# Seven block products for eight in the last FFN, and GpSimd sums for the first batch's inverse step

## The chip, the cores and the metric

One core of a Trainium2 chip runs the whole kernel. The metric is the time of one execution on the device, in microseconds (us), as a median of several executions. A profile shows one execution; its span is some 2 us shorter than the time reported for that same execution (2409.3 for 2411.47 us before), and executions of one kernel differ by a few us.

## The reference, cut to what matters

```python
# x, v: (4, 12544, 128); D = 128, d_ff = 768
h_filt = (np.maximum(pos_emb @ w1, 0.0) @ w2) * window[:, None]
y = irfft(rfft(x * v, 2 * S, axis=1) * rfft(h_filt, 2 * S, axis=0))[:, :S]   # long convolution
x = (x * y).reshape(B * S, D)                                               # 50176 tokens
h = np.maximum(np.maximum(x @ moe_w1, x @ moe_w2), x @ moe_w3)
return h @ moe_w_out
```

Everything is float32. The convolution of one batch is a chain of matrix products with constant tables; the FFN of one batch runs beside the convolution of the next. Only the FFN of the fourth batch runs alone.

## The kernel before

A batch's FFN has 32 tiles of 4 x 98 = 392 tokens. `t_last` makes the last inverse step of the convolution for a tile and multiplies by x; `up` makes one of six blocks of 128 hidden values; `down` multiplies it by w_out and adds up. The first of the three weight matrices is folded out: max(a, b, c) is written as a plus a maximum with differences, so `lin` carries the linear part and two up-products remain.

```python
def halves_mm(out, lhsT, rhs, start, stop):          # a product as two half-array products
    for h in range(2):
        nc.tensor.matmul(out[64 * h:64 * h + 64], lhsT[:, 64 * h:64 * h + 64], rhs, ...)

def t_last(i):                                       # i = (batch, tile)
    ...
    if i[0] == 0:                                    # batch 0: two 98-column products, accumulated
        for s in range(4):
            for c in range(2):
                halves_mm(y[:, s, :], zt[:, c, s * D:(s + 1) * D], f4[:, c, :], s == 0 and c == 0, c == 1)
    else:                                            # later: zt holds sums and differences of pairs of k1
        for s in range(4):
            for a in range(2):
                halves_mm(y[:, s, a * h:a * h + h], zt[:, a, s * D:(s + 1) * D], f4p[:, a, :], ...)
    ... # g = y * xT on VectorE

def up(i, f):
    halves_mm(pa[:, 0:N], w_sb[1][:, f * P:(f + 1) * P], rhs, True, True)
    nc.scalar.activation(h[:], pa[:, 0:N], Relu)
    halves_mm(pb[:, 0:N], w_sb[2][:, f * P:(f + 1) * P], rhs, True, True)
    nc.vector.tensor_tensor(out=h[:], in0=h[:], in1=pb[:, 0:N], op=ALU.max)
    return h

def down(i, f, h):
    if f == 0:
        halves_mm(pos_[i][:, 0:N], lin[:], gs[i], True, False)
    halves_mm(pos_[i][:, 0:N], wo_sb[:, f, :], h[:], False, f == NF - 1)
    ... # after the sixth: copy by ScalarE, DMA to outT from ScalarE's queue

for n, (b, i) in enumerate(tiles):                   # all 128 tiles
    for f in range(NF):
        ... # loads for tile n + 2
        h = up((b, i), f)
        if late is not None:
            down(*late)
        late = ((b, i), f, h)
        if f == 3 and n + 1 < len(tiles):
            t_last(tiles[n + 1])
        run(beside.pop(s, ()))                       # steps of the next batch's convolution
```

## Time and profile before

| | |
|---|---|
| time, median of 4 | 2414.89 us (2413.1 to 2417.17) |
| profiled span | 2409.3 us |
| TensorE busy | 99% |
| GpSimd busy, whole span / last batch's FFN | 13% / 0% |
| last inverse step of a tile, batch 0 / later | 1.36 / 0.92 us |
| period of a tile in the last batch | 13.44 us |

The prediction below shows the lines that carry this. A line of the chain of waits is "start, length, what"; a line of the table by stage is a stretch, its length, busy time of PE, PEld, DVE, ACT and POOL with instruction counts, the granted TensorE clock, DMA share and GB/s.

### The profile page before, as it was taken

Reading aid. Unit: us, or ns where it says so; the run is one execution under the profiler, and the core shown is the slowest. Engines: PE = TensorE matmul, PEld = TensorE weight load, DVE = VectorE, ACT = ScalarE, POOL = GpSimd, SP = SyncE. Lnnn points to the kernel's source line nnn. Section 1 sums busy time; section 2 is a strip of 40 time slices with the busy share of each in tenths; the row PEclk is TensorE's granted clock in tenths of the full one; section 3 lists DMA queues with packets and bytes.
Section 4 is the critical chain, followed back from the end, with each engine's and each line's share of the span. In section 5 each row is a group of like instructions: output and inputs, shape, how many; then the busy total and the mean of one; then the engine's idle time right before and its main releaser. Section 6 shows DMA issues by size and latency. Waiting matters only on the chain.

```text
span 2409.3 us, 63290 instructions
## 1 busy us (share of the span) xinstructions
PE 2393.4 (99%) x26089; PEld 1463.2 (61%) x26089; DVE 1286.4 (53%) x2719; ACT 1026.7 (43%) x1981; POOL 314.2 (13%) x349
## 2 busy tenths in 40 slices
PE   9999999999999999999999999999999999999999
PEld 8988866655555556666656546666665654444444
DVE  5588834466666645446666644446666642222222
ACT  2688834444444434444444424444444432222222
POOL 2022211011111101101111111101111100000000
PEclk9999999999999999999999999999999999999999
DMA  7778879767767659967777859968777742222221
GB/s 171 179 240 266 278 167 179 162 190 196 214 194 211 175 125 187 182 174 207 219 207 215 219 124 182 189 162 213 214 215 209 215 113 61 55 62 53 64 53 36
DMA packets 544553, 408.21 MB, mean 169 GB/s; under 512 B 390244, under 2 KB 436381, under 8 KB 544265
## 3 DMA queue, kind: packets, MB, share of 16 engines
q1 hardware_dynamic: 421760, 315.25, 53.8%
q10 hardware_dynamic: 117129, 74.31, 10.7%
q0 software_dynamic: 5376, 14.62, 2.1%
q8 instruction: 205, 3.36, 0.6%
q14 instruction: 83, 0.68, 0.1%
HBM read 295.76 MB, written 84.67 MB: 158 GB/s over the span
## 4 chain that ended last, share of the span: by engine, by line
PE 97%; DMA 1%; ACT 1%; DVE 0%; issue 0%; SPq 0%; ACTq 0%; POOL 0%; DVEq 0%
PE ops L132 24%; PE pb L132 21%; PE pa L132 21%; PE ps L132 13%; PE ps L141 7%; PE yps L132 5%; PE sps L688 3%; PE pm L303 1%; PE gps L674 1%; PE pst L341 1%; PE pw L132 1%; DMA hd<-ht 1%; ACT ht L693 0%; DMA xT<-in_x_dram 0%; DVE xt L424 0%
## 5 line engine op out<-in xcount | busy, mean ns | idle before, releaser
L548 DVE TENSOR_TENSOR hid<-hid,pb 128x392 f32<-128x392 f32 x768 | 431.8, 562 | 789.4 <-PE pb L132 510.2
L545 ACT ACTIVATE hid<-pa 128x392 f32<-128x392 f32 x768 | 381.9, 498 | 799.3 <-PE pa L132 630.1
L132 PE MATMUL pa<-gt,w_sb 128*64 128x392 f32 x3072 | 640.7, 493 | 1.1 <-DVE gt L533 1.1
L132 PE MATMUL pb<-gt,w_sb 128*64 128x392 f32 x3072 | 639.6, 492 | 1.4 <-ACT hid L545 1.2
L132 PE MATMUL ops<-hid,wo_sb 128*64 128x392 f32 x3072 | 639.5, 492 | 0.1
L132 PEld LDWEIGHTS pb<-gt,w_sb 128*64 128x64 f32 x3072 | 225.8, 137 | 283.0 <-issue 257.1
L132 PEld LDWEIGHTS ops<-hid,wo_sb 128*64 128x64 f32 x3072 | 227.1, 137 | 278.9 <-issue 228.8
L424 POOL TENSOR_TENSOR xt<-xt,xs 128x512 f32<-128x512 f32 x135 | 172.5, 1278 | 969.6 <-DVE xs L423 778.7
L132 PEld LDWEIGHTS pa<-gt,w_sb 128*64 128x64 f32 x3072 | 201.8, 137 | 111.3 <-issue 67.4
L141 PEld LDWEIGHTS ps<-f,uT 98*64 98x64 f32 x4096 | 178.0, 137 | 47.4 <-issue 44.7
L132 PEld LDWEIGHTS ps<-ab,wt 128*64 128x64 f32 x2880 | 168.4, 137 | 52.4 <-issue 26.8
L132 PE MATMUL ps<-ab,wt 128*64 128x128 f32 x2880 | 190.9, 274 | 1.8 <-DVE ab L431 1.7
L132 PEld LDWEIGHTS ps<-spec,wt 128*64 128x64 f32 x2880 | 168.0, 137 | 37.8 <-issue 34.2
L132 PE MATMUL ps<-spec,wt 128*64 128x128 f32 x2880 | 189.5, 273 | 1.4 <-issue 1.4
L141 PE MATMUL ps<-f,uT 98*64 98x90 f32 x4096 | 188.0, 241 | 0.0
L449 DVE TENSOR_TENSOR zs<-ps,z 128x256 f32<-128x256 f32 x270 | 102.0, 419 | 96.6 <-ACT z L447 94.3
L413 ACT ACTIVATE xs<-xt 64x512 f32<-64x512 f32 x180 | 113.1, 628 | 71.1 <-DVE xt L158 58.9
L431 DVE TENSOR_TENSOR ab<-xt 128x256 f32<-128x256 f32 x360 | 136.0, 419 | 1.6
L419 DVE TENSOR_TENSOR xt<-xt,ht 128x512 f32<-128x512 f32 x180 | 124.2, 690 | 15.6 <-ACT ht L693 15.2
L356 POOL COPY planes<-ut 128x784 uint16<-128x784 uint16 x90 | 76.2, 847 | 426.5 <-DVE ut L336 301.1
L145 ACT COPY spec<-ps 128x360 f32<-128x360 f32 (+1 forms) x132 | 71.8, 546 | 137.0 <-PE ps L141 136.8
L132 PEld LDWEIGHTS yps<-f4p,zt 90*64 90x64 f32 x3072 | 107.3, 138 | 34.4 <-issue 32.3
(86 smaller groups left out, 1824.4 us busy)
## 6 DMA issues: line engine op xcount, KB each, us to landing
wt<-wt_const SPq DMA_DIRECT2D x360, 256.0 KB, 4.8
ht<-hd SPq DMA_DIRECT2D x270, 256.0 KB, 4.5
zd<-zs ACTq DMA_DIRECT2D x180, 256.0 KB, 4.6
zt<-zd SPq DMA_DIRECT2D x192, 180.0 KB, 3.8
ut<-in_xr_dram SPq DMA_DIRECT2D x128, 196.0 KB, 3.6
ut<-in_vr_dram SPq DMA_DIRECT2D x128, 196.0 KB, 4.3
xT<-in_x_dram SPq DMA_DIRECT2D x512, 49.0 KB, 3.0
out_dram<-ot ACTq DMA_DIRECT2D x128, 196.0 KB, 4.0
```

The lines of the kernel that those rows point to most:

```text
L132: nc.tensor.matmul(out[64 * h:64 * h + 64], lhsT[:, 64 * h:64 * h + 64], rhs, start=start, stop=stop, skip_group_check=True)
L141: nc.tensor.matmul(ps[64 * c:64 * c + 64, 256 * i + r * N1:256 * i + (r + 1) * N1], a[:, r, :], table[:, c * N1:(c + 1) * N1], start=(i % ...
L145: copy(dst, ps[:].rearrange("p (s m) -> p s m", m=256)[:, :, 0:2 * N1].rearrange("p s (r k) -> p k r s", r=2))
L356: nc.gpsimd.tensor_copy(pl_[:, :, :, 0:NB], a[:].bitcast(U16).rearrange("p s (n h) -> p h s n", h=2))
L413: nc.scalar.mul(xs[0:64], xt[64:128], -1.0)
L419: nc.vector.tensor_tensor(out=xt[:], in0=xt[:], in1=hts[g][:, 0], op=ALU.mult)
L424: (nc.gpsimd if apart else nc.vector).tensor_tensor(out=xt[:], in0=xt[:], in1=xs[:], op=ALU.add)
L431: nc.vector.tensor_tensor(out=ab[:, :, q, :], in0=y[:, :, 0, :], in1=y[:, :, 1, :], op=op)
L449: nc.vector.tensor_tensor(out=zs[:, a], in0=ps[:, 0:256], in1=z1[:], op=op)
L545: nc.scalar.activation(h[:], pa[:, 0:N], Relu)
L548: nc.vector.tensor_tensor(out=h[:], in0=h[:], in1=pb[:, 0:N], op=ALU.max)
L688: nc.tensor.matmul(ps[64 * h:64 * h + 64, (2 * c + k) * 2 * D:(2 * c + k + 1) * 2 * D], G[:, k, c], w2x[:].rearrange("p s d -> p (s d)"), ...
```

## The change

First, batch 0's last inverse step is done as in the later batches. There the sums and differences of pairs of k1 (the index that this step sums over) come for nothing with an eviction; in batch 0 they are formed on the loaded tile, by GpSimd (by VectorE for the very first tile). Second, in the last batch's FFN two tiles go through w_out together as a 2 x 2 block product in Winograd's form, with seven products for eight; its sums of hidden tiles are GpSimd's work, its sums of weights are made once, by VectorE. To make room, some constants move to memory that is given back early, and the convolution's pools are closed before the last FFN. The start-up order changes a little too.

```diff
+    def t_sums(i, eng=nc.gpsimd):
+        if i[0]:
+            return
+        z0, z1 = zts[i]
+        even = hp.tile([N1, 512], FP32, tag="even", name="even", bufs=1)
+        eng.tensor_tensor(out=even[:], in0=z0, in1=z1, op=ALU.add)
+        eng.tensor_tensor(out=z1, in0=z0, in1=z1, op=ALU.subtract)
 ...
+    def s3(h, j): ...   # h11 - h21          def s2(h, j): ...   # h22 - s3
+    def s1(h, j): ...   # h21 + h22          def s4(h, j): ...   # h12 - s2      all on GpSimd
 ...
+        plan = (
+            (X, "h11", wo_sb[:, 0:NC, 0:64], True, None, [(copied, "p1", X)], None),
+            (Y, "s2", tw[:, 0], True, None, [(added, "u2", "p1", Y)], None),
+            (X, "h12", wo_sb[:, NC:, 0:64], False, (m1, first), [(copied, "c11", X)], None),
+            (Y, "s3", tw[:, 1], False, (m2, second_), [(added, "u3", "p1", Y)], None),
+            (X, "h21", wo_sb[:, 0:NC, 64:128], True, None, [(added, "c22", "u3", X)], None),
+            (Y, "h22", tw[:, 2], True, (linx[:], second_), [(added, "c21", "u3", Y)], (stored, 0)),
+            (X, "h12", wo_sb[:, NC:, 64:128], False, (m2, first), [(added, "c12", "u2", X)], (stored, 1)),
+        )       # per pair of tiles: 7 x 3 + 4 products of two halves of 196 columns
 ...
-    warm_up(30)
+    warm_up(22)
+    window_back()
+    warm_up(3)
 ...
-    op_ = ctx.enter_context(tc.tile_pool(name="op", bufs=2))
+    op_ = conv.enter_context(tc.tile_pool(name="op", bufs=2))
 ...      (the other pools of the convolution likewise)
+    first = up((B - 1, 0), 0)
     down(*late)
+    conv.close()
+    lp = ctx.enter_context(tc.tile_pool(name="lp", bufs=1))     # new hidden tiles, in that memory
```

More of the change, by code (lines that the diff above doesn't have):

```diff
@@ L66, in tables @@
     f32 = np.float32
-    return f1.astype(f32), f1h.astype(f32), f4.astype(f32), f4p.astype(f32), np.ascontiguousarray(both, f32)
+    return f1.astype(f32), f1h.astype(f32), f4p.astype(f32), np.ascontiguousarray(both, f32)
 @with_exitstack
@@ L103 @@
     zd = [dram.tile([N1, 2, 64, 256], FP32, name=f"zd{b}") for b in range(B)]
-    f1_t, f1h_t, f4_t, f4p_t, w_t = tables(NB)
+    f1_t, f1h_t, f4p_t, w_t = tables(NB)
     f1_d = nc.inline_tensor(f1_t, name="f1_const").ap()
     f1h_d = nc.inline_tensor(f1h_t, name="f1h_const").ap()
-    f4_d = nc.inline_tensor(f4_t, name="f4_const").ap()
     f4p_d = nc.inline_tensor(np.ascontiguousarray(f4p_t), name="f4p_const").ap()
@@ L113 @@
     eye_d = nc.inline_tensor(np.eye(P, dtype=np.float32), name="eye_const").ap()
-    w_sb = [const.tile([D, DFF], FP32, name=f"w_sb{i}") for i in range(3)]
+    w_sb = [None] + [const.tile([D, DFF], FP32, name=f"w_sb{i}") for i in (1, 2)]
     wo_sb = const.tile([P, NF, D], FP32, name="wo_sb")
     lin = const.tile([D, D], FP32, name="lin")
-    eye = const.tile([P, P], FP32, name="eye")
     f1 = const.tile([NB, 2 * N1], FP32, name="f1")
-    f4 = const.tile([N1, 2, NB], FP32, name="f4")
     spec = const.tile([P, N1, 2, D], FP32, name="spec")
@@ L226 @@
     pin = pro.enter_context(tc.tile_pool(name="pin", bufs=1))
+    eye = pin.tile([P, P], FP32, name="eye")
+    w_sb[0] = pin.tile([D, DFF], FP32, name="w_sb0")
     lwp = pro.enter_context(tc.tile_pool(name="lwp", bufs=3))
@@ L272 @@
     nc.gpsimd.dma_start(f1[:], f1_d)
-    nc.gpsimd.dma_start(f4[:], f4_d)
     nc.scalar.copy(winT[:, 0:64], warm[:, 0:64])
@@ L497, in t_load @@
         zt = hp.tile([N1, 2, 512], FP32, tag="zt", name="zt", bufs=2)
-        if b == 0:
+        for c in range(2):
             nc.sync.dma_start(
-                zt[:], zd[b][:, :, 2 * i:2 * i + 2, :].rearrange("k c t f -> k c (t f)"))
-        else:
-            for c in range(2):
-                nc.sync.dma_start(
-                    zt[NK * c:NK * c + NK],
-                    zd[b].rearrange("(g a) c t f -> g a c t f", a=2)[
-                        :, :, c, 2 * i:2 * i + 2, :].rearrange("g a t f -> g a (t f)"))
-        zts[b, i] = zt
+                zt[NK * c:NK * c + NK],
+                zd[b].rearrange("(g a) c t f -> g a c t f", a=2)[
+                    :, :, c, 2 * i:2 * i + 2, :].rearrange("g a t f -> g a (t f)"))
+        zts[b, i] = zt[:, 0], zt[:, 1]
         xT = hp.tile([D, 4, NB], FP32, tag="xT", name="xT", bufs=2)
@@ L511, in t_load @@
         xTs[b, i] = xT
+    def t_sums(i, eng=nc.gpsimd):
[5 more added lines that the diff above has]
+        eng.tensor_tensor(out=z1, in0=z0, in1=z1, op=ALU.subtract)
+        zts[i] = even[:], z1
     def t_last(i):
@@ L515, in t_last, with up @@
         ps = cps.tile([P, 512], FP32, tag="cv", name="yps")
-        g = hp.tile([D, 4, NB], FP32, tag="g", name="gt", bufs=2)
+        own = i[0] == B - 1 and i[1] > 1
+        g = (lp if own else hp).tile([D, 4, NB], FP32, tag="g", name="gt", bufs=4 if own else 3)
         y = ps[:, 0:N].rearrange("d (p n) -> d p n", p=4)
-        if i[0] == 0:
-            for s in range(4):
-                for c in range(2):
-                    halves_mm(y[:, s, :], zt[:, c, s * D:(s + 1) * D], f4[:, c, :],
-                              s == 0 and c == 0, c == 1)
-        else:
-            h = NB // 2
-            for s in range(4):
-                for a in range(2):
-                    halves_mm(y[:, s, a * h:a * h + h], zt[:, a, s * D:(s + 1) * D],
-                              f4p[:, a, :], s == 0 and a == 0, True)
-            y = y.rearrange("d p (a m) -> d p m a", a=2)
-        xT = xTs.pop(i)
-        if i[0] == 0:
-            nc.vector.tensor_tensor(out=g[:], in0=y, in1=xT[:], op=ALU.mult)
-        else:
-            nc.vector.tensor_tensor(out=g[:].rearrange("d p (m a) -> d p m a", a=2), in0=y,
-                                    in1=xT[:].rearrange("d p (m a) -> d p m a", a=2),
-                                    op=ALU.mult)
+        h = NB // 2
+        for s in range(4):
+            for a in range(2):
+                halves_mm(y[:, s, a * h:a * h + h], zt[a][:, s * D:(s + 1) * D],
+                          f4p[:, a, :], s == 0 and a == 0, True)
+        y = y.rearrange("d p (a m) -> d p m a", a=2)
+        xT = xTs.pop(i)
+        nc.vector.tensor_tensor(out=g[:].rearrange("d p (m a) -> d p m a", a=2), in0=y,
+                                in1=xT[:].rearrange("d p (m a) -> d p m a", a=2),
+                                op=ALU.mult)
         gs[i] = g
-    def up(i, f):
+    def up(i, f, tag="hid", bufs=3):
         rhs = gs[i][:].rearrange("d p n -> d (p n)")
-        h = hp.tile([P, N], FP32, tag="hid", name="hid")
+        h = (lp if tag[0] == "h" and tag != "hid" else hp).tile([P, N], FP32, tag=tag, name="hid", bufs=bufs)
         pa = hps.tile([P, 512], FP32, tag="hps", name="pa")
@@ L563, in down, with sum_, s3 @@
         nc.scalar.dma_start(dst, o[:])
+    H2 = N // 2
+    NC = NF // 2
+    ORDER = (("h11", 0), ("h21", 0), ("h11", 1), ("h22", 0), ("h21", 1), ("h11", 2),
+             ("h21", 2), ("h22", 1), ("h22", 2), ("h12", 0), ("h12", 1), ("h12", 2))
+    BUFS = {"h11": 3, "h21": 4, "h22": 4, "h12": 3}
+    NSTEP = len(ORDER)
+    LAG = 9
+    def sum_(out, a, b, op):
+        nc.gpsimd.tensor_tensor(out=out[:], in0=a[:], in1=b[:], op=op)
+    def s3(h, j):
+        h["s3", j] = lp.tile([P, N], FP32, tag="s3", name="s3", bufs=3)
+        sum_(h["s3", j], h["h11", j], h["h21", j], ALU.subtract)
@@ new lines, in s2, with s1, s4, products @@
+    def s2(h, j):
+        h["s2", j] = lp.tile([P, N], FP32, tag="s2", name="s2", bufs=3)
+        sum_(h["s2", j], h["h22", j], h["s3", j], ALU.subtract)
+    def s1(h, j):
+        sum_(h["h21", j], h["h21", j], h["h22", j], ALU.add)
+    def s4(h, j):
+        sum_(h["h12", j], h["h12", j], h["s2", j], ALU.subtract)
+    SUMS = {2: (s3, 0), 4: (s2, 0), 5: (s3, 1), 7: (s3, 2), 8: (s2, 1), 9: (s2, 2),
+            10: (s1, 0), 11: (s1, 1), 12: (s1, 2), 13: (s4, 0), 14: (s4, 1), 15: (s4, 2)}
+    def products(b, i, h, X, Y):
+        m1, m2 = lin[:, 0:64], lin[:, 64:128]
+        first, second_ = gs[b, i], gs[b, i + 1]
+        t = {}
+        def new(name, bufs=1):
+            return lp.tile([P, H2], FP32, tag=name, name=name, bufs=bufs)
+        def mm(ps, w, rhs, start):
+            for c in range(2):
+                nc.tensor.matmul(ps[64 * c:64 * c + 64, 0:H2], w, rhs[:, H2 * c:H2 * c + H2],
+                                 start=start, stop=True, skip_group_check=True)
+        def place(name):
+            if name[0] != "c":
+                t[name] = new(name)
+                return t[name][:]
+            n, m = int(name[1]) - 1, int(name[2]) - 1
+            if m not in t:
+                t[m] = lp.tile([P, 2, H2], FP32, tag="o", name="o", bufs=2)
+            return t[m][:, n]
+        def copied(name, ps):
+            nc.scalar.copy(place(name), ps[:, 0:H2])
+        def added(name, a, ps):
+            nc.vector.tensor_tensor(out=place(name), in0=t[a][:], in1=ps[:, 0:H2], op=ALU.add)
+        def stored(m):
+            dst = outT.rearrange("d (p b n) -> d p b n", b=B, n=NB)
+            for n in range(2):
+                for c in range(2):
+                    at = 4 * (i + n) + 2 * c
+                    nc.gpsimd.dma_start(
+                        dst[64 * m:64 * m + 64, at:at + 2, b, :],
+                        t[m][64 * c:64 * c + 64, n].rearrange("d (q n) -> d q n", q=2))
+        plan = (
[4 more added lines that the diff above has]
+            (X, "h21", wo_sb[:, 0:NC, 64:128], True, None, [(added, "c22", "u3", X)], None),
+            (Y, "h22", tw[:, 2], True, (linx[:], second_), [(added, "c21", "u3", Y)],
+             (stored, 0)),
+            (X, "h12", wo_sb[:, NC:, 64:128], False, (m2, first), [(added, "c12", "u2", X)],
+             (stored, 1)),
+        )
+        out = []
+        for ps, name, w, start, extra, then, store in plan:
+            for j in range(NC):
+                out.append([lambda ps=ps, name=name, w=w, start=start, j=j: mm(
+                    ps, w[:, j, :], h[name, j][:], start and j == 0)])
+            if extra:
+                out.append([lambda ps=ps, extra=extra: mm(ps, extra[0], extra[1][:].rearrange("d p n -> d (p n)"), False)])
+            out[-1] += [lambda a=a: a[0](*a[1:]) for a in then]
+            out[-1].append(store)
+        return out
@@ L610 @@
             mlp_in(i)
-        if i == 0:
-            window_back()
         if i:
@@ L750 @@
     hp = ctx.enter_context(tc.tile_pool(name="hp", bufs=3))
+    conv = ExitStack()
     f4p = hp.tile([N1, 2, NB // 2], FP32, name="f4p", bufs=1)
     nc.scalar.dma_start(f4p[:], f4p_d)
-    inq = ctx.enter_context(tc.tile_pool(name="inq", bufs=2))
+    inq = conv.enter_context(tc.tile_pool(name="inq", bufs=2))
     planes = [hp.tile([P, 2, 4, P], U16, name=f"planes{i}", bufs=1) for i in range(3)]
@@ L756 @@
         nc.gpsimd.memset(t[:].rearrange("p h s n -> p (h s n)"), 0)
-    op_ = ctx.enter_context(tc.tile_pool(name="op", bufs=2))
-    wp = ctx.enter_context(tc.tile_pool(name="wp", bufs=3))
-    hh = ctx.enter_context(tc.tile_pool(name="hh", bufs=3))
-    cvp = ctx.enter_context(tc.tile_pool(name="cvp", bufs=3))
-    cps = ctx.enter_context(tc.tile_pool(name="cps", bufs=4, space=PSUM))
+    op_ = conv.enter_context(tc.tile_pool(name="op", bufs=2))
+    wp = conv.enter_context(tc.tile_pool(name="wp", bufs=3))
+    hh = conv.enter_context(tc.tile_pool(name="hh", bufs=3))
+    cvp = conv.enter_context(tc.tile_pool(name="cvp", bufs=3))
     hps = ctx.enter_context(tc.tile_pool(name="hps", bufs=3, space=PSUM))
-    ops = ctx.enter_context(tc.tile_pool(name="ops", bufs=1, space=PSUM))
+    cps = conv.enter_context(tc.tile_pool(name="cps", bufs=4, space=PSUM))
+    ops = conv.enter_context(tc.tile_pool(name="ops", bufs=1, space=PSUM))
     state = {"turn": cps, "pair": (wp, hh), "cv": (cvp, cps), "xb": 3}
     tiles = [(b, i) for b in range(B) for i in range(NT)]
+    LAST = (B - 1) * NT
     late = None
-    for n, (b, i) in enumerate(tiles):
+    for n, (b, i) in enumerate(tiles[:LAST]):
         if i == 0:
             beside = {}
-            if b + 1 < B:
-                beside = conv_steps(b + 1, EARLY if b == 0 else 0)
+            beside = conv_steps(b + 1, EARLY if b == 0 else 0)
         if n == 0:
@@ L776 @@
             t_load(*tiles[1])
+            t_sums(tiles[0], nc.vector)
             t_last(tiles[0])
@@ L784 @@
                 t_load(*tiles[n + 1 + f])
+            if f == 1:
+                t_sums(tiles[n + 1])
             h = up((b, i), f)
@@ L788 @@
             late = ((b, i), f, h)
-            if f == 3 and n + 1 < len(tiles):
+            if f == 3:
                 t_last(tiles[n + 1])
+            if f == 5 and n + 1 == LAST:
+                t_last(tiles[n + 2])
             s = i * NF + f
@@ L794, with later @@
                 assert not beside, sorted(beside)
+    first = up((B - 1, 0), 0)
     down(*late)
+    conv.close()
+    lp = ctx.enter_context(tc.tile_pool(name="lp", bufs=1))
+    cps = ctx.enter_context(tc.tile_pool(name="cps2", bufs=3, space=PSUM))
+    ops = ctx.enter_context(tc.tile_pool(name="ops2", bufs=1, space=PSUM))
+    banks = [ops.tile([P, 512], FP32, name=f"ops{i}") for i in range(2)]
+    tw = lp.tile([P, 3, NC, 64], FP32, name="tw", bufs=1)
+    linx = lp.tile([D, 64], FP32, name="linx", bufs=1)
+    b11, b12 = wo_sb[:, 0:NC, 0:64], wo_sb[:, 0:NC, 64:128]
+    b21, b22 = wo_sb[:, NC:, 0:64], wo_sb[:, NC:, 64:128]
+    for out, a, b in ((tw[:, 1], b22, b12), (b12, b12, b11), (tw[:, 0], b22, b12),
+                      (tw[:, 2], b21, tw[:, 0]), (linx[:], lin[:, 0:64], lin[:, 64:128])):
+        nc.vector.tensor_tensor(out=out, in0=a, in1=b, op=ALU.subtract)
+    stream = {}
+    def later(step, fn, *args):
+        stream.setdefault(step, []).append((fn, args))
+    step, b = 0, B - 1
+    for i in range(0, NT, 2):
+        h = {}
+        X, Y = banks if i % 4 == 0 else banks[::-1]
+        for j, (name, f) in enumerate(ORDER):
+            n = int(name[1]) - 1
+            if j < 2 and i + 2 < NT:
+                t_load(b, i + 2 + j)
+            h[name, f] = first if step == 0 else up(
+                (b, i + n), f + (NC if name[2] == "2" else 0), name, BUFS[name])
+            if j == 0:
+                entries = products(b, i, h, X, Y)
+                for q, e_ in enumerate(entries):
+                    at_ = step + LAG + q * NSTEP // len(entries)
+                    for fn in e_:
+                        if isinstance(fn, tuple):
+                            later(at_ + 1, *fn)
+                        elif fn is not None:
+                            later(at_, fn)
+                for at_, (fn, c) in SUMS.items():
+                    later(step + at_, fn, h, c)
+            run(stream.pop(step, ()))
+            if j in (5, 8) and i + 2 < NT:
+                t_last((b, i + 2 + (j > 5)))
+            step += 1
+    for at_ in sorted(stream):
+        run(stream[at_])
 def kernel(x, v, pos_emb, w1, w2, moe_w1, moe_w2, moe_w3, moe_w_out):
```

## The prediction

> **What bounds the kernel now.** I read the page's busy shares first, then the chain of waits, then a table of busy time by stage (stage borders taken from when each batch's tiles start), then single pieces of the chain.
>
> ```profile
> PE 2393.4 (99%) x26089; PEld 1463.2 (61%) x26089; DVE 1286.4 (53%) x2719; ACT 1026.7 (43%) x1981; POOL 314.2 (13%) x349
> PE 97%; DMA 1%; ACT 1%; DVE 0%; issue 0%; SPq 0%; ACTq 0%; POOL 0%; DVEq 0%
> ```
>
> TensorE is 99% busy, and 97% of the chain that ends last is its own work. So only two things count: TensorE work removed, and new moments in which TensorE waits. The four stages in which an FFN runs (columns: stretch, length, then busy time of PE, weight load, DVE, ACT, POOL):
>
> ```profile
> 316.00:870.00 554.00, 552.18 (x5734) 326.97 (x5736) 307.00 (x661) 226.79 (x453) 79.44 (x71) 1.00 0.73 184
> 870.00:1412.00 542.00, 540.74 (x5844) 328.66 (x5842) 310.68 (x676) 231.66 (x464) 84.41 (x77) 1.00 0.79 193
> 1957.00:2410.00 453.00, 448.43 (x3578) 212.58 (x3573) 132.14 (x235) 116.33 (x235) 0.00 (x0) 1.00 0.22 57
> ```
>
> The first line is batch 0's FFN beside the convolution of batch 1, the last is the last batch's FFN alone. TensorE is busy all the time in each; in the last, GpSimd does nothing at all. The change touches exactly these two. From the chain of waits, in windows inside those stages (start, length, what; x32 counts matmul instructions, four to a pair of half-array fp32 products):
>
> ```profile
> 503.66 1.36 PE yps L132 x32
> 2051.07 0.92 PE yps L132 x32
> 2051.99 0.67 PE pa L132 x4
> 2052.66 0.66 PE pb L132 x4
> 2053.32 0.66 PE ops L132 x4
> 500.81 0.87 PE ps L132 x16
> 2064.51 0.92 PE yps L132 x32
> ```
>
> A 392-column pair costs 0.66 us (0.659 from the tile period below); four 128-column pairs cost 0.87, so 0.2175 each. The last inverse step of a tile ("yps") costs 1.36 us in batch 0, where two 98-column products per output are accumulated, but 0.92 us in later batches, where sums over k1 pairs were formed beforehand and the columns are 49. Tiles of the last batch follow each other by 2064.51 - 2051.07 = 13.44 us.
>
> **What the skill says.** "TensorE: Matmul & The Clock Gate", section "Wait — 56ns, not 53.3ns?", gives a warm matmul as columns over 2.4 GHz plus about 2.5 ns, and never less than about 25 ns however narrow. The trace agrees: 0.92/32 = 28.7 ns per instruction at 49 columns, more than the halving of 1.36 would give. So the first part saves less than its column count suggests. "GPSIMD Engine Reference", section "Elementwise — side-by-side cycle accounting", gives about 2.6 cycles per element for a two-input operation at 1.2 GHz; the 128x512 sum here takes 1278 ns, 2.5 ns per element with its start, which agrees. "SBUF — State Buffer", section "Who interferes with whom", says that a VectorE operation with two SBUF inputs and a GpSimd operation that reads SBUF block each other. The trace shows it rarely: VectorE's multiply on 128x512 is 685 ns in the median, 1353 at most.
>
> **Part 1, batch 0.** Removed: in each of 32 tiles 1.36 - 0.92 = 0.44 us of TensorE, on the path: **-14.1 us**. Added: two GpSimd sums of 90x512 per tile, 2 x 1.28 = 2.6 us in a tile of about 17 us (554/32); GpSimd goes from 79 to some 160 of 554 us. They are issued at f=1, the product that reads them at f=3: two steps and an up-product, some 6 us by the pieces above, against 2.6. The first tile's sums are on VectorE (2 x 0.69) at the stage's start, where the chain waits 4.69 us for xT; the second transfer for zt delays xT by some 0.5 us: **+0.7**. The split transfer is the one that later batches use, and there TensorE loses only 1.3 of 542 us. For sums blocked by VectorE and back I allow **+1**.
>
> **Part 2, last batch.** Before, two tiles cost 2 x 13.44 = 26.88 us: 38 pairs of 392 columns (24 for the two up-projections, 12 down, 2 linear) and two yps: (26.88 - 1.84)/38 = 0.659. After: the 24 up pairs and two yps stay, 24 x 0.659 + 1.84 = 17.66. Instead of 14 pairs of 392 there are 7 x 3 + 4 = 25 pairs of 196 columns. I have no 196-column pair in the trace; the filter products have 256 columns and give 1.73 us for 16 instructions, 0.4325 a pair. Between 0.2175 at 128 and 0.4325 at 256, 196 columns give 0.332. 25 x 0.332 = 8.30; sum 25.96; saved 0.92 a pair of tiles, x 16 = **-14.7 us**. That two halves with different moving data run beside each other as well as with the same is seen in the forward steps with 90 columns: 2.63 us for 64 instructions, 0.164 a pair; the rate of the 392-column pairs, 0.659/392 = 1.68 ns a column, gives 0.151.
>
> Twelve sums of 128x392 per pair of tiles go to GpSimd: 1278 x 392/512 = 0.98 us each, 11.7 us, plus eight DMA issues. GpSimd's issues here take 0.53 us with 64 rows and 0.78 for the 384-run load of w_out, so about 0.6 each: 4.8. Together 16.5 of 26 us: not the bound. By the order of the changed program most sums come several steps (of 2.16 us) before their product.
>
> **The switch of stages.** In the changed program's order of instructions and their waits, the first ScalarE write of the new hidden tiles and VectorE's first weight difference wait for the DMA of batch 2's last output tile, as the new pool takes its memory. That DMA takes 4.0 us after a 0.49 us copy. TensorE has three PSUM banks for up-products, so it runs about 2 us ahead and then stands some 3.4 us, and VectorE's five weight differences come after, some 0.8 more: **+4.2**, and 0.3 for restarting (the pa after the 4.69 us wait took 0.88 for 0.66).
>
> **The ends.** At the start five warm-up products go (16.11 us for 30, so 2.7), and the window's 1.1 us chain through ScalarE moves ahead of them; part is lost if pos_emb lands late, and that stretch is heavy with DMA: **-1.5**. At the end the last store is four GpSimd DMAs, one after the other, after four others: **+2**. Another **+1** for small waits in the last stage.
>
> Sum: -14.1 + 0.7 + 1 - 14.7 + 4.5 - 1.5 + 2 + 1 = -21.1; 2416.7 - 21.1 = **2395.6 us**, about 0.9% less.
>
> **Rivals.** (a) GpSimd becomes the bound of the last stage. For: it goes from 0 to over 60% busy, works in strict order, and its stores wait for VectorE in the middle of the sums; if each issue cost 1.2 us, the third s2 sum would come late once a pair of tiles, perhaps 1 us x 15: about 2410. Against: the measured issue times and the 26 us period. (b) The sums come late in batch 0: GpSimd stands behind a copy that waits for a transposing DMA (46 us of such waits, up to 6.4 each). Half the tiles losing 0.5 us would give back 8 of the 14: 2404. Against: these waits lie in the first quarter of the stage, and later planes copies start a few us apart with idle time between. (c) Everything hides: no wait at the switch, and the start gains its full 3.8 us: about 2386. Against: the wait stands in the program. (d) Narrow pairs cost more, 0.36 instead of 0.332, as more weight loads lie between: +0.7 a pair of tiles, +11: 2407. Against: 128-column pairs stream at 217 ns with the same number of loads.
>
> **Range and chances.** (c) sets the low end with a little over, 2384; (a), (b) or (d) alone end near 2404 to 2410, so 2409 is the high end. Faster by over 2% means under 2368.4, that is 48 us, while the whole TensorE work removed is below 33 with the start: 0.02. Slower by over 2% (2465) needs a bound that no row shows: 0.02. Within 2%: 0.96.
>
> **What would show it.** Batch 0's yps pieces at 0.92 in place of 1.36, and its stage near 540 us with TensorE over 99% busy. In the last stage a period of 26.0 us per two tiles, the narrow products at 0.33 a pair, GpSimd at 60 to 65%, sums of 0.98 us. One TensorE wait of 3 to 5 us at the switch, released by ScalarE or VectorE behind an output DMA. It is wrong if TensorE's waits for GpSimd sums add up to over 5 us in either stage, if a 196-column pair is far from 0.33, or if the wait at the switch is absent.

## The result

The changed kernel takes 2398.22 us (median of 4, 2395.2 to 2400.77) against 2414.89 in the same rounds. The ratio is 0.993, 95% interval 0.9913 to 0.9947. Ratios here are the mean time of one kernel's fast runs over that of the other's of the same rounds, so not quite the ratio of the medians. That is 16.7 us less by medians; the two profiled spans differ by 14.5.

The page of the changed kernel, busy shares and the chain that ended last:

```profile
PE 2366.7 (99%) x26773; PEld 1506.3 (63%) x26773; DVE 1317.7 (55%) x2806; ACT 1020.1 (43%) x1981; POOL 659.8 (28%) x730
PE 96%; DMA 1%; issue 1%; POOL 1%; ACT 1%; DVE 0%; SPq 0%; ACTq 0%; POOLq 0%; DVEq 0%
```

TensorE's busy time fell by 2393.4 - 2366.7 = 26.7 us, and the span by only 14.5. So about 12 us came back as time in which TensorE did nothing, and the chain now has shares of "issue" and POOL that it did not have. The table by stage of the changed kernel, batch 0's FFN and the last batch's after its first pairs:

```profile
318.00:860.00 542.00, 540.67 (x5714) 322.05 (x5712) 310.84 (x661) 226.25 (x453) 157.85 (x133) 0.99 0.77 189
2000.00:2395.00 395.00, 386.75 (x3854) 238.14 (x3850) 138.65 (x284) 97.15 (x206) 255.17 (x307) 0.99 0.23 55
```

GpSimd went from 79 to 158 us in batch 0's stage and from nothing to 255 of 395 us in the last. TensorE is still full in both. The chain of waits of the changed kernel, in a window of batch 0 and one of the last batch (ops L604 are the new products, eight instructions to two of them):

```profile
433.71 0.92 PE yps L130 x32
2213.18 0.92 PE yps L130 x32
...
2215.44 0.66 PE ops L604 x8
...
2222.31 0.99 PE ops L604 x12
...
2239.15 0.92 PE yps L130 x32
```

Batch 0's step is at 0.92 us. A 196-column product takes 0.66/2 = 0.33 us, and two tiles take 2239.15 - 2213.18 = 25.97 us against 26.88. Both steady-state savings came as worked out. What TensorE waited for, from the table of its waits (total, times, longest):

```profile
PE pb L130 <- ACT hid L541: 4.6, 4, 3.2
PE pm L302 <- issue: 3.6, 1, 3.6
PE yps L130 <- DVE even L513: 2.2, 1, 2.2
...
PE ops L604 <- POOL s L574: 1.5, 2, 0.9
```

Each of these stands at a border between stages: the switch to the last FFN, the first MLP step, the FFN's first tile, the last pair of tiles. Cutting both spans at the same events gives the ledger:

| stretch | before | after | difference | predicted |
|---|---|---|---|---|
| start to the FFN's first up-product | 319.24 | 321.05 | +1.8 | -0.8 (-1.5 + 0.7) |
| from there to batch 1's first yps | 549.81 | 538.74 | -11.1 | -13.1 (-14.1 + 1) |
| to the last batch's first yps | 1101.36 | 1101.58 | +0.2 | 0 |
| to the end | 438.89 | 433.43 | -5.5 | -7.2 (-14.7 + 4.5 + 2 + 1) |
| sum | 2409.30 | 2394.80 | -14.5 | -21.1 |

**The FFN's start.** The next two fences are the same line of the table by stage, 310 to 330 us, of the kernel before and of the changed one; the number after the five busy times is the granted clock.

```profile
310.00:330.00 20.00, 17.96 (x212) 11.08 (x212) 4.92 (x9) 5.18 (x14) 0.06 (x1) 1.00 0.75 173
```

```profile
310.00:330.00 20.00, 16.38 (x162) 9.85 (x163) 4.69 (x8) 3.97 (x13) 5.24 (x5) 0.83 0.56 133
```

The clock was full before and 0.83 on average after. The changed kernel's chain of waits in that window shows it piece by piece:

```profile
313.41 3.54 DMA zt<-zd
...
317.03 0.70 DVE even L513
...
317.76 0.70 DVE zt L514
...
318.50 1.76 PE yps L130 x28
...
321.05 1.58 PE pa L130 x4
322.63 1.31 PE pb L130 x4
323.94 1.31 PE pa L130 x4
```

A pair that takes 0.66 us elsewhere takes 1.31 here, twice as long, and the first inverse step takes 1.76 for 0.92. The same two pieces at the ends of this stretch in the chain of the kernel before:

```profile
319.24 0.88 PE pa L132 x4
...
322.09 1.32 PE ops L132 x8
```

From the first up-product to the end of the first two down-products the changed kernel needs 6.25 us (321.05 to 327.30), the kernel before 4.17 (319.24 to 323.41): 2.1 us lost, and 0.8 before them. TensorE had waited 2.21, 0.38 and 0.82 us around there; in the kernel before the waits were 0.68 and 1.14. The clock record falls at 318.45, before the third of these waits, and comes back at 325.28.

The +1.8 of the first row is another matter. The changed kernel and the runs below that equal it up to this point reach the first up-product at 321.05, 322.75, 318.92 and 320.14 us; the second and the last of these are one and the same kernel. So a difference of 1.8 us between two single profiles there can be chance. The mean granted clock, too, was 1.000 in the profiled execution before, but 0.998 or 0.999 in 24 of the 27 runs of that kernel that were timed with the experiments (0.995 to 0.997 in the four of the changed one). So the clock falls in most of them as well; where, be it after the last product, no trace shows.

**The switch.** The changed kernel's chain at the border to the last FFN:

```profile
1968.51 0.68 PE ops L130 x4
1969.21 0.49 ACT ot L557
1969.73 3.83 DMA out_dram<-ot
...
1973.81 0.51 ACT hid L541
...
1974.36 1.57 PE pb L130 x4
1975.93 1.31 PE pa L130 x4
1977.24 0.77 PE pb L130 x4
```

The chain leaves TensorE for the copy and DMA of batch 2's last output tile, and comes back through the first write of a new hidden tile. TensorE itself ran three more products (1.98 us) in that time and waited 3.2 us. Then the slow clock again: 0.91 + 0.65 + 0.11 + 0.05 (the next pa took 0.71) = 1.7 us.

**The end.** Before, the last product ended at 2405.5 and the span at 2409.3. After, it ends at 2388.2 and the span at 2394.8: 2.7 us more. TensorE also waited 1.5 us for a sum of the last pair, while before it waited 0.7 for VectorE.

### The profile page after: what moved, and what is told of

The parts are those of the page before. It is cut to its first block, busy times and chain, and to the rows that moved or that the text cites. A ratio compares the mean times of both kernels' runs of the same rounds, so it can differ in the third digit from the quotient of the medians.

```text
span 2394.8 us, 65342 instructions
## 1 busy us (share of the span) xinstructions
PE 2366.7 (99%) x26773; PEld 1506.3 (63%) x26773; DVE 1317.7 (55%) x2806; ACT 1020.1 (43%) x1981; POOL 659.8 (28%) x730
## 4 chain that ended last, share of the span: by engine, by line
PE 96%; DMA 1%; issue 1%; POOL 1%; ACT 1%; DVE 0%; SPq 0%; ACTq 0%; POOLq 0%; DVEq 0%
PE pb L130 21%; PE pa L130 21%; PE ops L130 18%; PE ps L130 13%; PE ps L139 8%; PE ops L604 5%; PE yps L130 5%; PE sps L777 3%; PE pm L302 1%; PE pst L340 1%; PE gps L763 1%; DMA specH<-in_pos_emb_dram 1%; POOL out_dram L628 0%; DMA zd<-zs 0%; DMA hd<-ht 0%
## 5 line engine op out<-in xcount | busy, mean ns | idle before, releaser
L130 PE MATMUL ops<-hid,wo_sb 128*64 128x392 f32 x2304 | 481.5, 492 | 0.0
L130 PEld LDWEIGHTS ops<-hid,wo_sb 128*64 128x64 f32 x2304 | 173.6, 137 | 205.7 <-issue 162.1
L130 PEld LDWEIGHTS yps<-f4p,zt 90*64 90x64 f32 x3584 | 134.5, 139 | 25.9 <-issue 22.9
L130 PE MATMUL yps<-f4p,zt 90*64 90x49 f32 x3584 | 137.7, 222 | 0.4 <-DVE zt L514 0.4
```

## The experiments

Each of the kernels gave a correct result. Runs of one call share their runs of the kernel before, whose median was 2415.85 in the first call, 2415.76 in the second and 2413.05 in the third, so I compare ratios across calls.

### Each part alone

The first kernel keeps the seven products and undoes batch 0's part (the diff is put in words):

```diff
-        zts[b, i] = ... sums on GpSimd, 49-column products with f4p
+        if i[0] == 0: 98-column products with f4, both halves of k1 accumulated (as before)
```

> The seven products in the last batch, batch 0 with the old 98-column step (yps 1.36 us, no sums). Theory (two separate parts, and the last batch gives most of its gain back at its two ends): about 5.5 us less than before, span near 2404, with the TensorE wait of about 5 us at the switch and the slow tail still there. Rival (the ledger of the prediction: 14.7 gained, 7.5 given back): about 7 us less. Second rival (the parts disturb each other through GpSimd): over 10 us less when alone.

Measured: 2412.99 us, ratio 0.9994, interval 0.9982 to 1.0006. That is no gain that can be told from zero, less than every theory had said. Its profile says where the gain went. From the last batch's first yps to the end it takes 435.4 us, 3.5 less than before. Its TensorE waited up to 3.7 us at the switch, and five pieces after it ran slow (1.58, 1.31, 1.31, 1.31, 0.81 for 0.66: 3.0 us). And though it has no sums, its FFN starts slowly too, as the table by stage of this kernel shows:

```profile
310.00:330.00 20.00, 16.30 (x161) 9.59 (x162) 3.33 (x6) 4.01 (x10) 2.73 (x3) 0.83 0.78 169
```

It reaches batch 1's first yps 3.3 us later than the kernel before (872.35 against 869.05). Its waits there were 1.53 us for zt and 2.12 for xT. So the slow clock is not a matter of the sums, nor of the split transfer for zt, which this kernel does not have in batch 0. Why TensorE waits longer here for the first loads than in the kernel before stays open.

The second kernel keeps the sums and undoes the last batch's part (all 128 tiles in the old loop):

```diff
-    for n, (b, i) in enumerate(tiles[:LAST]): ...    # then the seven products
+    for n, (b, i) in enumerate(tiles): ...           # the old loop to the end
```

> The sums over k1 pairs in batch 0, the last batch as before (eight products). Theory: 32 x 0.44 = 14.1 us less TensorE work, given back in part at the start of the FFN, where the first tile's loads, sums and the slowed clock cost about 4 us: about 9.5 us less than before, span near 2400; every yps piece of batch 0 at 0.92 us. Rival (prediction: only 0.7 lost there): 12.5 us less. With the products-only run the two should add up to what both do together.

Measured: 2402.83 us, ratio 0.995, interval 0.9938 to 0.9962: 12.1 us less by the ratio. It lies between the theory (9.5) and the prediction's ledger (12.5), nearer the latter; the profiled span, 2401.1, is 8.2 less. Its FFN starts with the same slow pieces (1.58, 1.31, 1.31, 1.31). The gains by ratio of the two parts alone, 1.4 and 12.1, make 13.5; both together make 16.9. The difference lies within the intervals, so no hindrance shows. That each alone pays for the slow start, which both together pay once, would fit, but is not shown.

### The start as before

```diff
-    warm_up(22)
-    window_back()
-    warm_up(3)
+    warm_up(30)
 ...
+        if i == 0:
+            window_back()
```

> The changed kernel with the warm-up and the window chain of the kernel before (30 products, chain inside the first MLP step). Theory: the first MLP product starts near 18.2 to 18.7 us whatever stands before it, so no difference from the changed kernel beyond 1 us; the 3.4 us pause before it shrinks to about 1. Rival (prediction): 1.5 us slower than the changed kernel.

Measured: 2398.95 us, ratio 0.9938, interval 0.9925 to 0.9951, against 0.993 for the changed kernel: no difference that the runs show, but their intervals would not show 1.5 us either. The chains of the changed kernel and of this one, in the window around the first MLP step:

```profile
15.25 3.41 issue
18.66 1.39 PE pm L302 x19
```

```profile
14.94 1.73 PE pw L130 x16
16.67 1.30 issue
17.97 2.04 PE pm L302 x45
```

With five warm-up pairs fewer the pause before the first MLP product grows, and that product does not start earlier. It starts between 17.83 and 19.01 us in all twelve profiles, although pos_emb has landed at 15.3. What ends the pause is not in the profile; that stays open. In the longer pause the clock falls as well: from 18.0 to 21.5 us it is 0.51 in the changed kernel and 1.00 in this one and in the kernel before. The last MLP product ends at 38.45 us in the changed kernel, 38.26 in this one and 38.41 in the kernel before. So the prediction's 1.5 us do not show by then, though single profiles could hide some of them: the other nine end it between 37.90 and 39.85.

### The switch without its wait

```diff
-    op_ = conv.enter_context(tc.tile_pool(name="op", bufs=2))
+    op_ = ctx.enter_context(tc.tile_pool(name="op", bufs=2))      # and opened ahead of the others
```

The two output tiles keep their memory, so the new hidden tiles lie where nothing waits for an output DMA.

> The changed kernel, but the memory of the output tiles is not given to the new pool at the switch, so its first writes wait for no output DMA. Theory: the TensorE wait of 5.2 us at the switch shrinks below 1.5 us and the pieces after it run at 0.66 instead of 1.57, 1.31 and 0.77: 5 to 6.5 us less than the changed kernel. Rival (three PSUM banks and VectorE's five weight differences make the wait): the wait stays above 3 us and the time moves by under 2 us.

Measured: 2391.87 us, ratio 0.9906, interval 0.9893 to 0.9918, against 0.9913 to 0.9947 for the changed kernel: 5.8 us less by the ratios (the second measurement below makes it 4.3). The chain of this kernel at the switch:

```profile
1969.67 0.66 PE pa L130 x4
1970.33 0.66 PE pb L130 x4
1970.99 0.66 PE pa L130 x4
...
1976.25 0.92 PE yps L130 x32
```

No gap and no slow piece. From the last batch's first yps to its third it takes 1976.25 - 1961.87 = 14.38 us, the changed kernel 1980.69 - 1961.37 = 19.32: 4.94 us, the 3.2 of waiting and the 1.7 of slow clock. VectorE's five weight differences and the three PSUM banks are the same in both, so they did not make the wait. The DMA did; this is shown.

The slow clock, however, does not always follow. The kernel with 14 fill products (see below) has the same switch, and TensorE waits 3.1 us there, but its clock stays at 1.00:

```profile
1976.01 0.88 PE pb L130 x4
1976.89 0.66 PE pa L130 x4
```

From the last batch's first yps to its third it takes 17.87 us, so the switch costs 3.5 us there. In the kernel with the products only, where TensorE waited 3.7 us and the clock then stayed low for 6.8 us instead of 3.4, it takes 21.13 us, so the cost is 6.7.

### Stores from another queue

```diff
-                    nc.gpsimd.dma_start(
+                    nc.sync.dma_start(
```

> The changed kernel, with the last batch's 128 stores issued from SyncE's queue in place of GpSimd's. Theory: the stores stand in GpSimd's order before the last sums and after the last of all; taken away, the TensorE wait of 1.5 us for the third s2 sum of the last pair goes, and the 6.6 us from the last product to the end shrink to about 4: 3 to 4 us less than the changed kernel, GpSimd down from 65% to some 47% of the last stage. Rival (the end is set by the landing of the stores, whoever issues them): under 1.5 us less.

Measured: 2394.62 us, ratio 0.9911, interval 0.9896 to 0.9926. GpSimd falls from 65% (232.72 of 360 us between 2000 and 2360) to 46% (166.86). The chain of the changed kernel at the end, then that of this one:

```profile
2375.60 1.23 POOL out_dram L628 x2
2376.83 2.24 issue
...
2380.28 1.03 POOL s L574
...
2381.36 1.57 PE ops L604 x16
```

```profile
2378.29 6.66 PE ops L604 x80
```

The third s2 sum no longer stands behind a store that paused for 2.24 us, and the last twenty products run without a gap. (That pause is there in every profile with GpSimd's stores, before the third of these stores for 2.24 us, or before the second for 2.41; why, the profile does not show.) But the end did not come nearer: from the last product to the end it is 7.4 us where the changed kernel has 6.6. So from the last batch's first yps the gain is 433.4 - 432.4 = 1.0 us. The theory was right on the wait and wrong on the end; the rival fits the end better. The rest of the difference lies before the last batch in the profiled run, where runs differ by chance; the intervals of the timed runs overlap.

### TensorE kept busy at the FFN's start

```diff
             t_sums(tiles[0], nc.vector)
+            pw = cps.tile([P, 512], FP32, tag="cv", name="pw")
+            for _ in range(14):                      # 8 in the later kernel
+                halves_mm(pw[:, 0:256], w_sb[1][:, 0:P], w_sb[2][:, 0:256], True, True)
             t_last(tiles[0])
```

> The changed kernel, with 14 pairs of 256-column products (0.43 us each, results unused) between the fold and the first tile's step, so that TensorE does not idle for 5 us there. Theory: the first pieces after the wait run slow (1.58, 1.31, 1.31 in place of 0.66, the first step 1.76 in place of 0.92) as the clock fell in the wait; kept busy they run at full speed: about 2.5 to 3 us less than the changed kernel, with the same waits for the loads. Rival (they are slow because their weights or data arrive late): no change, the pieces stay at 1.3 to 1.6 us.

Measured with 14: 2396.39 us, ratio 0.9916, interval 0.9901 to 0.9931. The first pieces run at 0.88, 0.66, 0.66, so the clock was the cause of the slow ones. But 14 were too many: they end at 321.03, and only then does the first inverse step start.

> As the kept-warm run, but 8 pairs of unused products in place of 14, as the 14 ran 2.4 us past the arrival of the loads (they end at 321.03 and the first step starts there). Theory: the fill ends near 318.4, within 0.5 us of when the sums are ready, the first pieces run at 0.66 to 0.9 us, and the time is 2 to 3 us under the changed kernel. Rival (the clock's fall costs nothing on the path): no difference.

Measured with 8: 2394.39 us, ratio 0.9928, interval 0.9914 to 0.9941. The chain of this kernel and its line by stage:

```profile
314.07 3.45 PE pw L130 x32
317.52 0.94 PE yps L130 x32
...
319.26 0.88 PE pa L130 x4
320.14 0.66 PE pb L130 x4
```

```profile
310.00:330.00 20.00, 19.15 (x234) 12.70 (x235) 6.55 (x12) 4.25 (x10) 5.83 (x6) 1.00 0.68 166
```

The mechanism is shown: with TensorE busy the clock stays at 1.00, and the 2.1 us of slow pieces are gone: from the first up-product to batch 1's first yps it takes 536.7 us in all four runs with a fill, and 538.7 in the changed kernel. In the timed runs, which spread over 5.8 us, the gain cannot be told from zero against the changed kernel's 0.993.

### All together

All three changes at once, with the fill of 14:

> The three together: output tiles' memory kept, stores from SyncE's queue, TensorE kept busy at the FFN's start. Theory: they act in three places and add up, 6 + 3.5 + 2.5 = 12 us less than the changed kernel, near 2386 us, 1.2% under the kernel before. Rival (a gain in one place is lost in the next): 6 to 8 us less.

Measured: 2393.06 us, ratio 0.9904, interval 0.9888 to 0.9921. The gains did not add up to 12: by the medians it is 5.2 us under the changed kernel, no more than the kept memory gives alone. The fill overran again (it ended at 322.99), and the stores gained only the 1 us above. The second attempt has the fill of 8, and the stores of the last pair split between SyncE and ScalarE:

```diff
+            last = i == NT - 2
-                    nc.gpsimd.dma_start(
+                    (nc.scalar if last and c else nc.sync).dma_start(
```

> Output tiles' memory kept at the switch, the fill of 8, and the stores from SyncE's queue, the last pair's split between SyncE and ScalarE. Theory: 5 to 6.5 from the switch, 2 to 3 from the fill, 1 to 3 at the end: near 2388 us, and 3 us or more under the run with the memory kept alone. Rival (gains are lost in the next wait): no better than that run.

Measured: 2389.30 us, ratio 0.9907, interval 0.9893 to 0.992; three of its four runs lie between 2388.28 and 2390.08, one at 2393.8. On the same chip, the kernel with only the output tiles' memory kept ran again:

> The kernel with only the output tiles' memory kept, once more on the same chip as the best one, for a direct comparison: 2391 to 2393 us as before, TensorE's wait at the switch under 1.5 us again.

Measured: 2391.87 us, ratio 0.9912, interval 0.9898 to 0.9926; TensorE's longest wait for the new hidden tiles is 0.6 us again. The combined kernel has the lowest median of all, 2.6 us under that one, but the intervals overlap: the further gain is not established by the timed runs. Cut at the same events, its profile is 1.5 us shorter in batch 0's stretch and 1.0 in the last than that of the repeat, as the fill and the stores would give, and 1.2 us longer before the first up-product, where runs differ by chance. Its last product ends at 2379.2 and its span at 2386.7. Its last store has landed at 2382.6, and 4.0 us follow in which the trace has next to nothing. In the kernel before, the last transfer was issued at 2406.06 and had landed at 2408.3, so 1.0 us followed. What the program's end waits for there stays open.

## Why the prediction was right

It said 2395.6 us, 2384 to 2409; measured are 2398.22. The nearness owes something to luck: the prediction started from 2416.7 us, where the kernel before took 2414.89 in these rounds, so of the change itself it had 21.1 us for 16.7. Point by point:

- **Part 1's saving: right.** 0.44 us a tile is measured at the piece. Without the slow clock's 2.1 us the stretch of batch 0 is 11.1 + 2.1 = 13.2 us shorter, as it is in the runs with the fill, for 31 x 0.44 = 13.6 that lie in it. No TensorE wait for a GpSimd sum shows in that stage, so rival (b) is refuted; sums and VectorE do hold each other up at times (a multiply took 1639 ns at most, for 1353 before, and the three longest each began some 0.2 us after a sum), but TensorE lost nothing by it. One reading of the skill was loose: by the rule that the prediction quotes, 49 columns would take about 23 ns (an estimate), or its least of 25, and the trace has 28.7, so it agrees only in being more than half of the time of 98 columns.
- **Part 2's saving: right.** 25.97 us a pair of tiles for 25.96 predicted, 0.33 us a product for 0.332. Rivals (a) and (d) are refuted in the steady state: GpSimd is 65% busy and TensorE waits for none of its sums until the last pair.
- **The switch: right in mechanism, 4.9 for 4.5 us, with the parts mis-sized.** The wait itself was 3.2 us for 3.4. The 0.8 us for the weight differences did not show, and the restart cost 1.7 us for 0.3. That the sum fits is in part luck: the same switch cost 3.5 us in one other run and 6.7 in another, with the clock. Rival (c) is refuted by the wait.
- **The FFN's start: the term that failed most.** Predicted +0.7; measured are 2.1 us of slow pieces, which the runs with the fill show to be the clock's, and +1.8 before the first up-product, which holds the start-up too and may be chance. The sums and the later load came as described; what was left out is the clock. The prediction read the 4.69 us of the DMA for xT as a wait, and the 0.88 us of the first piece after it as the price of a restart. But TensorE had other work meanwhile and waited only 0.68 and 1.14 us. That was the case in which the clock had not fallen.
- **The start-up: failed.** -1.5 predicted, no gain shows by the end of the MLP, since the first MLP step does not start earlier and its clock falls.
- **The end: +2 predicted;** measured 2.7 us more from the last product to the end, and 0.8 more waiting (1.5 for the last pair's sum, less 0.7 before), which the prediction had put down as 1 us of small waits.

The two misses at the start, 4.7 us together (1.8 + 2.1 for -0.8, the 1.8 perhaps by chance), and 1.7 us at the last batch's borders make up nearly all of the difference between the ledger's -21.1 and the profile's -14.5.

## What to carry to other kernels

When one engine is busy all the time, the steady part of a change can be worked out to some tenths of a microsecond from the lengths of its pieces in the chain (25.97 us a pair of tiles for 25.96, 13.2 a batch for 13.6); the errors sit at the borders between stages, so look there for memory that changes hands and name the transfer that must land first. A saving that is limited to one stage must pay for that stage's two borders: here the seven products alone gained 14.6 us in the steady state and nothing in the total that can be told from zero. Not reusing the memory of two small tiles took the wait at one of these borders away, and gave 4 to 6 us in the kernel with both parts. A short wait of TensorE costs more than its length when the clock falls after it, and whether it falls can differ from run to run; unused products in the wait kept the clock up here, but no more of them should run than the wait holds.

## What the Trainium skill lacked or had wrong

- "TensorE: Matmul & The Clock Gate", section "HAM oscillation — how this bites in real kernels", gives the rule of no idle gaps over about 3.4 us. Shorter ones were enough here. Between 315.04 and 318.45 us of the changed kernel TensorE works 0.87 us, its longest wait is 2.21 us, and the clock is 0.50 from 318.45 on (1.31 for 0.66 us a piece). In the kernel with the products only 1.8 us of idle time between 315.0 and 318.4 were enough; in the run with 14 fill products 2.0 us between 1974.0 and 1977.4 were not. Every low stretch in these traces that ends before its program does lasts 3.4 or 6.8 us.
- "GPSIMD Engine Reference", section "Elementwise — side-by-side cycle accounting": its 2.6 cycles per element hold (1.28 us at 512 elements, 1.02 at 392: 2.1 ns an element), but its row for what each instruction costs has no time for GpSimd; these two leave about 0.2 us.
- "DMA: Bandwidth & Descriptors", section "Specifications", gives a first-byte latency of about 1 us for GpSimd's queue and 0.6 for the others. No run here shows the first byte by itself; from issue to landing the same stores of 49 KB took 2.1 us in the median from either queue, so no difference between the queues shows. A store took 0.60 us of the issuing engine's time on GpSimd and 0.61 in SyncE's queue.
- No page that we found explains the pause before the first MLP product (0.8 to 3.9 us, ended by nothing that the profile shows), the 2.24 us pause between two of GpSimd's DMA issues, or why 4.0 us pass between the last landing and the end of the program in the combined kernel and 1.0 in the kernel before.
